# Mask rows of batch 1 from one pair's rows, and another order of work behind the opening

## The chip, the cores and the metric

The kernel runs on one core of a Trainium2 chip. The core has a matmul engine (PE, whose weight loads the profile lists apart as PEld), VectorE (DVE), ScalarE (ACT), GpSimd (POOL) and SyncE (SP), which issues the DMA transfers. Each engine works through its own queue in order and waits on semaphores for the others. PE writes its results to PSUM; DVE and ACT read them from there, GpSimd works in SBUF only. The metric is the device time of one execution in microseconds (us), the median of several runs.

## The reference

The computation is a block-sparse attention followed by a feed-forward layer. There are 4 batches, 8 heads, 768 positions and 64 columns per head, in 24 blocks of 32 positions:

```python
scores = scale * np.matmul(q, k.transpose(0, 1, 3, 2))
mask = np.abs(blk_i - blk_j) <= window            # window = 1
mask = mask | (blk_i == 0) | (blk_j == 0) | (blk_i == n_blocks - 1) | (blk_j == n_blocks - 1)
for qb in range(n_blocks):
    for kb in sampled_blocks[qb]:
        mask[qb*block:(qb+1)*block, kb*block:(kb+1)*block] = True
attn = softmax(np.where(mask, scores, -1e9))
x = (attn @ v)                                    # as 3072 rows of 512
h = x @ w_in                                      # 1024 columns
solu = h * softmax(h)
ln = (solu - mean) / sqrt(var + 1e-6) * g_ln
out = ln @ w_out                                  # 3072 x 512
```

The mask is the same for all batches and heads.

## The kernel before

**Tiling.** The heads are taken in four pairs. For each batch `b`, three query tiles `t` of 256 rows and each pair, `attend` makes three scores (each of four matmuls with 256 columns, called parts below), three exponentials on ACT of 128x1024 (L557), and one `pv` of 24 matmuls into an accumulator bank of PSUM (`mbank`, two banks); DVE takes reciprocals (L581) and writes the normalised rows (`norm`, L584). When four pairs of a tile are there, the rows are turned (`turn_x`, by a transposing DMA, `cross_x`, or on PE) and two row tiles of 128 go through `feed`: eight matmuls with `w_in` (L631), an exponential with its sum (L651), the product `us` (L654), statistics on DVE (L661, L664), a turn by DMA (`cross_u`, L738), eight matmuls with `w_out` (L748) and a scale (L758) that empties the accumulator bank into `ots`, which is stored. Row tiles are numbered through, from 0 to 23.

**The mask** is part of the matmul. kT and qT, the turned k and q, have 64 rows of data and 24 more rows (`MC`): for k, which block a column belongs to; for q, a negative number for each block that its row must not see. There are two kT and two qT, for even and odd batches. Batch 0's mask rows come with its turns on PE, pair by pair. Batch 1's were copied from batch 0's by two DMAs of SBUF to SBUF (`m1dma`, L800 for k and L801 for q), 24 partitions of 12,288 bytes each, when all four pairs' turns of batch 0 are copied out of PSUM. Batches 2 and 3 write only the data rows, so the mask rows stay.

**k, q and v.** In batch 0 k and q are cast to bf16, turned on PE and copied out by DVE or ACT (the opening). In later batches (`crossed`) a pair's k or q is loaded in float32, cast to bf16 (`cast6`, L270), turned by a DMA (`cross_kq`, L523) and put into kT or qT by two copies on DVE (`split`, L270). v is loaded and cast (`cast6`, L270).

**The weights.** w_in is loaded in four quarters (two for each half of its columns) and cast in eight pieces (`wcast`). w_out is loaded in two halves; `wg` (L425) multiplies its rows by the gain vector, which PE has turned (L407) and one copy has put into `g_sb`; PE sums those (L434), and eight folds `wo` (L439) write the final w_out.

**The order.** No loop sets the order of the work. The program first collects 1149 steps, each with its engine, what it depends on and which buffers it takes and frees; then the list `ORDER` puts all of them in one row, and `ENGINES` moves some steps to another engine than the default. Each engine issues its own steps in that order, and waits where its operands or its buffer are not there. Buffers (`take`) are given out in that order too, so a step that comes earlier can take another buffer. 26 `spare` matmuls on constants fill PE in the opening.

Of the kernel before, what the change touches and what calls it, by code (L numbers as in the profile page):

```python
# [11 lines left out]
ACT = mybir.ActivationFunctionType  # L12
# [7 lines left out]
    "ACT": [9, 24, 127, 291, 543, 1070, 1072, 1114, 1118, 1121],  # L20
    "DVE": [89, 92, 93, 95, 96, 126, 134, 135, 143, 161, 162, 165, 389, 393, 412, 420, 622, 626, 630, 639, 653,
        863, 868, 885, 886, 1116],
# [114 lines left out]
def kernel(  # L137
# [11 lines left out]
    nc = tc.nc  # L149
# [3 lines left out]
    NB = S // BLK  # L153
    NR = sampled_blocks.shape[1]
    P = 128
    NCH = S // P
# [696 lines left out]
```

## Time and profile before

| | |
|---|---|
| Median of 3 runs | 207.79 us (207.52 to 208.26) |
| Profiled execution | 206.38 us, with a span of 204.4 us from its first to its last instruction |
| PE busy | 198.4 us (97%) |
| ACT busy | 174.0 us (85%) |
| DVE busy | 149.9 us (73%) |
| GpSimd busy | 58.0 us (28%) |
| Granted PE clock | 1.00 |
| DMA | 43.17 MB, mean 211 GB/s |

A busy engine in this table is one with an instruction in it; matmuls are pipelined, so a busy PE is not PE at its peak. In rows of the profile, "out<-in" are names of buffers, "x24" is a count, and the brackets at the end of a row give the idle time before it and what ended it. A row of SP is the issue of a transfer, not the transfer. Times in rows count from the start of the span.

### The profile page before, as it was taken

To read this page: it belongs to the slowest core of one execution; us is meant where nothing else is said; L and a number is where in the kernel's file an instruction comes from. 1 tells how busy PE (TensorE), PEld (TensorE's weight loads), DVE (VectorE), ACT (ScalarE), POOL (GpSimd) and SP (SyncE) were. 2 spreads that over 40 slices of the span, in tenths; PEclk is the share of its full clock that TensorE was granted. 3 is DMA by queue.
4 is the path that set the end of the run, shared out by engine and by line. 5 is a ranking of instruction groups with operands and counts; after the bars stand their busy time and mean duration, and the time that the engine had idled before them with its cause. 6 is when DMAs were issued, how large, how long until landed. Compare 5 with 4: busy or idle time off the path is not lost.

```text
span 204.4 us, 5699 instructions
## 1 busy us (share of the span) xinstructions
PE 198.4 (97%) x2269; PEld 141.3 (69%) x2298; DVE 149.9 (73%) x341; ACT 174.0 (85%) x219; POOL 58.0 (28%) x132
## 2 busy tenths in 40 slices
PE   8999999999999999999999999999999999999993
PEld 4689886777657768667767777667677686675452
DVE  3488697999979648959776776599849736686771
ACT  4699999988998999999899899979998997775751
POOL 5705403430133024222303415025040110032160
PEclk9999999999999999999999999999999999999999
DMA  5999999989999999889999989999970921327524
GB/s 141 327 373 362 386 380 265 145 137 246 197 215 322 265 247 228 170 192 256 224 274 228 289 203 275 154 232 228 235 211 5 211 45 32 74 103 157 154 81 180
DMA packets 72214, 43.17 MB, mean 211 GB/s; under 512 B 53316, under 2 KB 67148, under 8 KB 72140
## 3 DMA queue, kind: packets, MB, share of 16 engines
q1 hardware_dynamic: 72152, 42.81, 86.8%
q8 instruction: 18, 0.29, 0.6%
q14 instruction: 8, 0.07, 0.1%
q10 hardware_dynamic: 36, 0.00, 0.0%
HBM read 23.07 MB, written 6.29 MB: 144 GB/s over the span
## 4 chain that ended last, share of the span: by engine, by line
PE 82%; DVE 9%; DMA 4%; issue 1%; POOL 1%; ACT 0%; POOLq 0%; SPq 0%; DVEq 0%
PE s L551 26%; PE mbank L748 17%; PE h L631 15%; PE mbank L572 15%; PE h L464 3%; DMA qx<-qb 2%; DVE us L654 2%; PE h L812 2%; DMA vst<-in_v_dram 2%; DVE w_out_sb L439 1%; PE mbank L812 1%; DVE ots L758 1%; DVE ex L425 1%; PE mbank L771 1%; DVE qT L270 1%
## 5 line engine op out<-in xcount | busy, mean ns | idle before, releaser
L557 ACT ACTIVATE ex<-s 128x1024 bf16<-128x1024 f32 x144 | 141.0, 1025 | 16.1 <-PE s L551 13.8
L551 PE MATMUL s<-qT,kT 88*128 88x256 bf16 x576 | 82.8, 272 | 0.2
L551 PEld LDWEIGHTS <-kT 88*128 88x128 bf16 x576 | 52.8, 97 | 20.9 <-issue 0.5
L748 PE MATMUL mbank<-w_out_sb,uTs 128*128 128x512 bf16 x171 | 45.4, 379 | 0.6
L631 PE MATMUL h<-w_in_sb,xT 128*128 128x512 bf16 x170 | 45.2, 378 | 0.7
L572 PEld LDWEIGHTS <-ex 128*128 128x128 bf16 x1152 | 40.9, 97 | 4.1 <-DVE ots L758 0.5
L572 PE MATMUL mbank<-va,ex 128*128 128x65 bf16 x1152 | 42.3, 193 | 0.3 <-DVE ots L758 0.2
L654 DVE TENSOR_TENSOR us<-h,e 128x1024 bf16<-128x1024 f32 x22 | 26.9, 1221 | 4.5 <-ACT e L651 4.3
L661 DVE BATCH_NORM_STATS2 bs<-us 128x6 f32<-128x512 bf16 x44 | 28.9, 682 | 0.2
L631 PEld LDWEIGHTS <-xT 128*128 128x128 bf16 x192 | 18.5, 97 | 13.9
L748 PEld LDWEIGHTS <-uTs 128*128 128x128 bf16 x184 | 17.3, 97 | 13.1
L758 DVE TENSOR_SCALAR ots<-mbank,rs 128x512 f32<-128x512 f32 x22 | 16.4, 746 | 11.1 <-POOL rs L703 4.5
L651 ACT ACTIVATE e<-h 128x1024 bf16<-128x1024 f32 x22 | 22.6, 1029 | 1.3 <-POOL vr L670 1.3
L581 DVE RECIPROCAL r<-mbank 128x4 f32<-128x4 f32 x48 | 8.1, 172 | 21.1 <-PE mbank L572 20.9
L670 POOL TENSOR_SCALAR vr<-z,mv 128x1 f32<-128x1 f32 x22 | 6.4, 293 | 58.2 <-DVE mv L664 50.5
L584 DVE TENSOR_TENSOR x<-mbank,r 128x256 bf16<-128x256 f32 x48 | 20.1, 421 | 1.2
L703 POOL TENSOR_TENSOR rs<-vr,neg_half 128x1 f32<-128x1 f32 x24 | 13.9, 579 | 1.5
L270 POOL CAST kb<-kst 128x768 bf16<-128x768 f32 x8 | 6.8, 854 | 21.4 <-DMA kst<-in_k_dram 19.8
L270 POOL CAST qb<-qst 128x768 bf16<-128x768 f32 x8 | 6.9, 858 | 11.9 <-DMA qst<-in_q_dram 10.4
L270 POOL CAST va<-vst 128x768 bf16<-128x768 f32 x8 | 6.8, 850 | 11.8 <-DMA vst<-in_v_dram 9.8
L667 POOL TENSOR_TENSOR z<-z 128x1 f32<-128x1 f32 x22 | 4.3, 197 | 19.0 <-ACT e L651 19.0
L270 DVE COPY kT<-kc 64x768 bf16<-64x768 bf16 x24 | 8.3, 348 | 0.6 <-DMA kc<-kb 0.3
(109 smaller groups left out, 133.8 us busy)
## 6 DMA issues: line engine op xcount, KB each, us to landing
vst<-in_v_dram SPq DMA_DIRECT2D x16, 384.0 KB, 4.9
out_dram<-ots SPq DMA_DIRECT2D x23, 256.0 KB, 2.3
kst<-in_k_dram SPq DMA_DIRECT2D x15, 384.0 KB, 5.7
qst<-in_q_dram SPq DMA_DIRECT2D x12, 384.0 KB, 5.6
w_out_f<-in_moe_w_out_dram SPq DMA_DIRECT2D x2, 1024.0 KB, 11.2
qst<-in_q_dram SPq DMA_DIRECT2D x4, 256.0 KB, 7.3
uTs<-in_moe_w_in_dram SPq DMA_DIRECT2D x2, 512.0 KB
ots<-in_moe_w_in_dram SPq DMA_DIRECT2D x2, 512.0 KB, 7.2
```

The source lines that it names most:

```text
L270: (nc.vector if o.eng == "DVE" else nc.gpsimd).tensor_copy(out=dst, in_=src)
L551: nc.tensor.matmul(s[:, m, :], kT[i][0:KR, pr, jc, hh, :], qT[i][0:KR, pr, 2 * t : 2 * t + 2, hh, :], start=(m % 2 == 0), stop=(m % 2 == 1))
L557: exs.append(op("exp", "ACT", lambda o, so=so: nc.scalar.activation(out=exb[o.slot], in_=lay["s"][so.slot], func=ACT.Exp, scale=scale), [s ...
L572: nc.tensor.matmul(acc(o)[:, qt, hh, :], exb[exs[n].slot][:, m, qt * P : (qt + 1) * P], va[i][:, 2 * pr + hh, jc, :], start=first, stop=(n ...
L584: nrm = op("norm", "DVE", lambda o: nc.vector.tensor_tensor(out=xb[x_of[b, t].slot][:, :, 2 * pr * D : (2 * pr + 2) * D].rearrange("p a (h ...
L631: nc.tensor.matmul(hx(n), xTb[xt[0].slot][:, qt, c, :], w_in_sb[n][:, c, :], start=(c == 0), stop=(c == KD - 1))
L651: zs = op("silu_e", "ACT", lambda o: nc.scalar.activation(out=eb[o.slots["e"]], in_=lay["h"][0].rearrange("p a f -> p (a f)"), func=ACT.Ex ...
L654: us = op("mult", "DVE", lambda o: nc.vector.tensor_mul(out=ub[o.slot], in0=lay["h"][0].rearrange("p a f -> p (a f)"), in1=eb[zs.slots["e" ...
L661: bs.append(op("stats", "DVE", lambda o, n=n: nc.vector.bn_stats(out=bsb[(bs[0] if bs else o).slot][:, n, :], in_=ub[us.slot][:, w(o, n)]) ...
L703: rs = op("rs", "POOL", lambda o: nc.gpsimd.tensor_tensor(out=rsb[o.slot], in0=vrb[vr.slot], in1=neg_half, op=ALU.pow), [vr, c2], take="rs ...
L748: nc.tensor.matmul(mbank[m0.slot], uTb[ut[0].slot][:, KF // 2 * n + f, :], w_out_sb[n][:, f, :], start=(n == 0 and f == 0), stop=(n == 1 a ...
L758: nc.vector.tensor_scalar(out=otb[o.slot], in0=mbank[os_[0].slot], scalar1=rsb[rs.slot], scalar2=None, op0=ALU.mult)
```

## The change

It has three parts.

1. **The mask copies.** Both still have 288 KB to write. The source is now only the first pair's rows, read four times (a broadcast over the pairs), so each copy has 96 runs of 3,072 bytes instead of 24 of 12,288. The k copy waits for the two copies out of PSUM of the first pair's k, the q copy for the first pair's two and for the mask step, not for all pairs'.
2. **Engines.** 18 steps go from DVE to GpSimd: four of the w_in casts, two casts of batch 0's q, three v casts of batch 0, and nine casts of later batches (among them batch 1's first q and its v of pairs 0 and 3). Ten go from GpSimd to DVE: three w_in casts, two casts of batch 0's q, and five of later batches (among them batch 1's first k and its v of pair 2). The copy of the gain vector and the scales of row tiles 14, 15 and 19 go from DVE to ACT, the last scale from ACT to DVE.
3. **The order** from the 81st of 1149 steps to the 624th. Behind that it is the same. The number of steps and of PE instructions does not change.

SP's queue shows most of the new order. From the load of batch 0's last q on it was: w_in quarter (second half), w_in quarter (first), v of pair 3, w_in quarter (first), w_in quarter (second), both w_out halves, then batch 1: q0, k0, k1, k2, q1, **mask q**, q2, turns of k0 and q0, turn of x tile 1, turn of q1, **mask k**, turn of k1, turn of us 1, loads k3, q3, turns of q2, k2, turn of us 2, **load v0**, turn of x tile 2, turn of k3, turn of q3, loads v1, v2, v3. It is now: w_in quarter (first), v of pair 3, w_out half (chunks 4 to 7), w_in quarters (first, second, second), other w_out half, then batch 1: k0, k1, q0, q1, k2, turn of k0, load q2, turns of q0 and of x tile 1, **mask k, mask q**, turn of q1, load k3, turn of k1, load q3, turn of us 1, turns of q2, k2, turn of us 2, turn of k3, turn of x tile 2, **load v0**, turn of q3, loads v1 and v2, and, behind a k load of batch 2 and the turn of us 3, v3.

On DVE, the w_out folds stand behind the reciprocal and norm of the first batch's pv (tile 1, pair 2) instead of around them; the statistics' closing steps come later. On PE the gain vector's turn comes ahead of the score of pair 2 and some scores change places; the kinds and numbers of matmuls are the same.

```diff
 ENGINES = {
     "POOL": [7],
-    "ACT": [9, 24, 127, 291, 543, 1070, 1072, 1114, 1118, 1121],
-    "DVE": [89, 92, 93, 95, 96, 126, 134, 135, 143, 161, 162, 165, 389, 393, 412, 420, 622, 626, 630, 639, 653,
-        863, 868, 885, 886, 1116],
+    "ACT": [9, 24, 100, 127, 291, 543, 811, 826, 1032, 1070, 1072, 1114, 1118],
+    "DVE": [86, 87, 89, 90, 126, 135, 153, 168, 385, 411, 412, 626, 657, 867, 876, 885, 886, 1116],
 }
 ORDER = [
...
-    1134, 97, 178, 135, 137, 138, 1141, 139, 140, 144, 26, 181, 42, 189, 1133, 179, 30, 29, 146, 145, 187, 148,
-    190, 188, 153, 185, 147, 1125, 36, 162, 186, 150, 149, 194, 151, 38, 143, 43, 44, 163, 196, 195, 191, 39,
+    1134, 97, 178, 135, 137, 138, 1141, 139, 140, 144, 26, 29, 145, 98, 181, 42, 30, 153, 189, 179, 146, 1125,
+    190, 187, 147, 148, 185, 36, 38, 1133, 188, 43, 44, 99, 149, 150, 162, 186, 194, 163, 39, 164, 195, 151, 143,
...
-            mask1["k"] = op("m1dma", "SP", lambda o: nc.sync.dma_start(out=kT[1][MC], in_=kT[0][MC]), kdone)
-            mask1["q"] = op("m1dma", "SP", lambda o: nc.sync.dma_start(out=qT[1][MC], in_=qT[0][MC]), qdone + [mq0])
+            for nm, t, done in (("k", kT, kdone[:2]), ("q", qT, [qdone[0], qdone[NPR], mq0])):
+                mask1[nm] = op("m1dma", "SP", lambda o, t=t: nc.sync.dma_start(
+                    out=t[1][MC].rearrange("r a c h p -> r a (c h p)"),
+                    in_=t[0][MC, 0:1].rearrange("r a c h p -> r a (c h p)").broadcast_to([NB, NPR, NCH * 2 * P])), done)
```

98 rows, old and new, of the table ORDER are left out of this document.

## The prediction

> **What bounds the kernel now.** I read the page first, then the engines by stage, then what PE waits for. The page:
>
> ```profile
> span 204.4 us, 5699 instructions
> PE 198.4 (97%) x2269; PEld 141.3 (69%) x2298; DVE 149.9 (73%) x341; ACT 174.0 (85%) x219; POOL 58.0 (28%) x132
> ```
>
> The busy time by stages (columns: stretch, length, then each engine's busy time):
>
> ```profile
> 7.00:30.00 23.00, 22.91 (x348) 20.36 (x351) 18.48 (x50) 21.25 (x23) 8.70 (x14) 1.00 1.05 369
> 30.00:62.00 32.00, 31.58 (x339) 21.84 (x344) 29.04 (x60) 29.63 (x37) 8.72 (x16) 1.00 1.05 208
> 62.00:96.00 34.00, 33.52 (x399) 24.00 (x401) 25.61 (x58) 31.58 (x39) 10.13 (x21) 1.00 1.06 235
> 96.00:180.00 84.00, 83.25 (x981) 59.64 (x993) 59.70 (x133) 74.96 (x89) 19.72 (x44) 1.00 0.82 182
> ```
>
> PE never rests for long, at a granted clock of 1.00. From 30 to 62 us DVE and ACT are at 29 of 32 as well; behind that DVE falls to 60 of 84. The PE instructions are the same before and after, so the change can win only what PE waits behind the opening, and lose whatever new waits it makes. Those waits (what PE's weight loads wait for, total, times, longest):
>
> ```profile
> PEld L572 <- DVE ots L758: 0.5, 1, 0.5
> PEld L551 <- DVE kT L270: 0.3, 1, 0.3
> PEld L572 <- issue: 0.3, 1, 0.3
> PEld mbank L407 <- issue: 0.2, 1, 0.2
> ```
>
> They sum to 1.3 us: hardly more can be won.
>
> **The change, part by part.**
>
> *DVE from 34 to 57 us.* Two of the waits are for DVE, so its queue is the term. Two weight folds (L439) stretched under GpSimd casts, and two casts that leave DVE:
>
> ```profile
> 36.11 0.55 DVE L270 CAST qb<-qst 128x768 bf16<-128x768 f32 x1
> 37.23 1.31 DVE L439 SCALAR_TENSOR_TENSOR w_out_sb<-w_out_f,g_sb,wbar 128x512 bf16<-128x512 f32 x1
> 36.90 1.10 POOL L270 CAST qb<-qst 128x768 bf16<-128x768 f32 x1 [0.97 <-DMA qst<-in_q_dram]
> 39.61 1.16 DVE L439 SCALAR_TENSOR_TENSOR w_out_sb<-w_out_f,g_sb,wbar 128x512 bf16<-128x512 f32 x1
> 39.40 0.83 POOL L270 CAST kb<-kst 128x768 bf16<-128x768 f32 x1 [1.41 <-DMA kc<-kb]
> 43.72 0.72 DVE L439 SCALAR_TENSOR_TENSOR w_out_sb<-w_out_f,g_sb,wbar 128x512 bf16<-128x512 f32 x1
> 57.21 0.56 DVE L270 CAST va<-vst 128x768 bf16<-128x768 f32 x1 [0.32 <-DMA vst<-in_v_dram]
> ```
>
> A fold takes 0.72 alone, 1.31 and 1.16 under a cast: 0.59 + 0.44 = 1.03 lost. Both ended 0.54 behind the cast's end (38.54 against 38.00, 40.77 against 40.23): the cast made them wait. Batch 1's first q cast (0.55) goes to GpSimd, its first k cast comes to DVE earlier, in this hole:
>
> ```profile
> 31.68 0.18 DVE L581 RECIPROCAL r<-mbank 128x4 f32<-128x4 f32 x1 [1.28 <-PE mbank L572]
> 35.50 0.69 DVE L661 BATCH_NORM_STATS2 bs<-us 128x6 f32<-128x512 bf16 x1
> 35.88 0.88 PEld L572 LDWEIGHTS <-ex 128*128 128x128 bf16 x24
> ```
>
> The hole of 1.28 covers it (0.55); without the hole it would cost 0.55. In the new order DVE takes a reciprocal right behind these statistics, which end at 36.19; it needs the pv whose weight loads end at 36.76 and whose result comes a little later, with the folds queued behind. That is 0.7 of new idle time. Sum: -0.55 - 1.03 + 0.7 = -0.9 if no fold meets a cast. Two k/q casts of batch 1 (pairs 2) now fall on GpSimd near 40 us, by the landing of their transposes; each that meets a fold costs 0.44 to 0.59. I take one, the middle of none and two: DVE is 0.4 earlier, with ends 0.9 earlier and 0.1 later (a third collision counts another 0.5).
>
> *The wait at 56.94.* The last splits of pair 2, and what PE does:
>
> ```profile
> 56.17 0.72 DVE L270 COPY kT<-kc 64x768 bf16<-64x768 bf16 x2
> 55.97 0.64 PEld L748 LDWEIGHTS <-uTs 128*128 128x128 bf16 x4
> 56.94 0.33 PEld L551 LDWEIGHTS <-kT 88*128 88x128 bf16 x4 [0.33 <-DVE kT L270]
> 59.03 0.64 PEld L631 LDWEIGHTS <-xT 128*128 128x128 bf16 x4
> 59.78 0.53 PEld L551 LDWEIGHTS <-kT 88*128 88x128 bf16 x4
> ```
>
> The splits end at 56.89, 0.4 earlier would be 56.5. PE needs about 0.11 to turn from a 512-column group to a score (59.67 to 59.78), so of 0.33 some 0.2 can go: **-0.2** (ends -0.2 and +0.1).
>
> *The wait at 62.84.* A pv waits for an accumulator bank that DVE empties late (scale of row tile 1):
>
> ```profile
> 61.09 0.99 PEld L572 LDWEIGHTS <-ex 128*128 128x128 bf16 x24
> 62.03 0.75 DVE L758 TENSOR_SCALAR ots<-mbank,rs 128x512 f32<-128x512 f32 x1
> 62.84 0.78 PEld L572 LDWEIGHTS <-ex 128*128 128x128 bf16 x24 [0.48 <-DVE ots L758]
> ```
>
> Ahead of that scale the v cast of 57.21 (0.56) leaves DVE, and DVE starts 0.4 earlier: it ends near 61.8 instead of 62.78, while PE, 0.2 ahead and with one more score (about 0.35) in front of that pv, arrives near 62.5. **-0.47** (ends -0.47 and 0). What is late next is v itself, the first rival below.
>
> *The other two waits.* The gain vector's turn (L407) moves ahead into the opening, where PE waits anyway for DVE and ACT: 0, ends -0.2 and 0. The 0.3 at L572 near 42 us: DVE and ACT meet there in both orders: 0, ends -0.3 and +0.3.
>
> *Gain vector's copy on ACT.* 0.17 on DVE:
>
> ```profile
> 22.05 0.17 DVE L270 COPY g_sb<-mbank 128x8 f32<-128x8 f32 x1 [1.07 <-PE mbank L407]
> 44.38 2.85 ACT L557 ACTIVATE ex<-s 128x1024 bf16<-128x1024 f32 x3 [0.85 <-PE s L551]
> ```
>
> ACT is at 21.25 of 23 up to 30 us, so some 0.2 may show there, but at 44.38 ACT has 0.85 to spare: 0, ends 0 and +0.2 without that cover.
>
> *w_in and w_out loads and casts.* One w_out half now loads ahead of three w_in quarters, four w_in casts go from DVE to GpSimd and three come back. The bytes in front of batch 1's loads are the same. GpSimd's price:
>
> ```profile
> L270 POOL CAST w_in_sb<-ots 128x512 bf16<-128x512 f32 x3 | 1.8, 614 | 3.0 <-PE h L464 2.3 <-DMA ots<-in_moe_w_in_dram 0.7
> ```
>
> Four such casts now run beside DVE's casts for the first feed and may hold one of them for most of 0.61; the hole of 1.28 comes only behind that feed. 0, since DVE has the three casts in front of its last w_out products, ends 0 and +0.4.
>
> *Mask copies.* Two transfers:
>
> ```profile
> 26.55 0.87 SPq L801 DMA_DIRECT2D qT<-qT  x1
> 42.17 0.78 SPq L800 DMA_DIRECT2D kT<-kT  x1
> 47.48 1.04 PE L551 MATMUL s<-qT,kT 88*128 88x256 bf16 x8
> vst<-in_v_dram SPq DMA_DIRECT2D x16, 384.0 KB, 4.9
> ```
>
> Both now issue behind the transpose of x tile 1, near 38 to 41 us; a 384 KB load lands in 4.9, so these 288 KB are there by 46, ahead of the first score of batch 1 (47.48). The bytes stay; fewer sources to wait for changes nothing, because the q copy, waiting for all pairs, was already issued at 26.55. SP still pays two issues (0.87 and 0.78). 0, ends -0.1 and +0.3; past 47.5 each us of delay would be a us of PE.
>
> *Late parts.* Three scales (0.75 each on DVE) go to ACT late in the run, where ACT has time to spare (74.96 of 84): 0, end +0.3. The last scale goes from ACT to DVE:
>
> ```profile
> 199.27 0.75 DVE L758 TENSOR_SCALAR ots<-mbank,rs 128x512 f32<-128x512 f32 x1 [0.50 <-PE mbank L748]
> 201.15 0.47 ACT L779 ACTIVATE ots<-mbank,rs 128x256 f32<-128x256 f32 x1 [0.54 <-PE mbank L771]
> ```
>
> Half of DVE's columns take about 0.42 (estimate from 0.75 for 512 and a fixed part): **-0.05**, ends -0.1 and 0. Behind 62 us six casts leave DVE and four come; DVE has 8 us to spare in 34 there, so 0.
>
> *Sum.* -0.2 - 0.47 - 0.05 = -0.7. The profiled execution took 206.38 (2.0 around its span of 204.4), 1.4 below the median of the three runs, 207.79; it becomes 205.7, and the median 207.1.
>
> One rule speaks against the change. The Trainium skill (SBUF — State Buffer, Who interferes with whom) says that VectorE and GpSimd share a port pair under an exclusive lock, and that whoever starts first holds it for the whole instruction while the other blocks. The two folds that ended 0.54 behind their casts agree with it. By it, every cast moved to GpSimd can hold DVE for its whole 0.83 instead of the 0.5 I count, and with two such on the folds the sum would be near 0 instead of -0.7.
>
> **The rivals.**
>
> *Slower: v of batch 1 comes late.* SP's queue here:
>
> ```profile
> 53.26 0.57 SPq L353 DMA_DIRECT2D vst<-in_v_dram  x1
> 54.01 1.24 SPq L614 DMA_TRANSPOSE xT<-x  x1
> 55.35 1.26 SPq L523 DMA_TRANSPOSE kc<-kb  x1
> ```
>
> The first v load of batch 1 moves behind these two transposes, which wait for DVE's casts, splits and norms. Its cast now sits on GpSimd, in order, and others wait behind it. With everything else in place it issues at 53.26 + 2.5 = 55.8, lands 4.9 later at 60.7, and is cast (0.83) at 61.5; PE wants it at 60.9. I count on the transposes' issuing about 1 us earlier, because DVE is earlier: issue 54.6, cast by 60.4. It costs from an issue at 55.2 on (60.9 - 0.83 - 4.9), eats the whole gain of 0.7 at 55.9, and is worth +0.6 at 56.5: 208.4. For it: DMA is full here (1.05 of its engines). Against: before, that v was cast at 57.77, 3.3 us ahead of PE.
>
> *No change: the collisions eat DVE's lead.* Two or three folds and products meet casts, DVE is 0.2 to 0.7 late at the splits, and the wait at 56.94 grows by as much as the one at 62.84 loses; or feed 0 is 0.4 late. 0 to -0.2: 207.7. For it: DVE at 29.04 of 32. Against: fewer casts on DVE.
>
> *The mask copies matter by themselves.* If the 26.55 copy held up the loads and transposes of batch 1, up to 1 us of DVE's start would come forward; but PE could win only the waits above, 1.3 in all: 206.5. It is the low end.
>
> **How the numbers follow.** Forecast (both DVE waits shortened) 0.44, with the mask case in it; no change 0.22; slower 0.34, by late v mostly, since PE, ACT, DVE and SP are all nearly full from 30 to 62 us and any of them being late costs. About 0.3%, 0.6 us, is what a measurement of this kernel can tell from no change; 207.1 lies just past it, so faster 0.44, same 0.22, slower 0.34. The range goes from 206.4 (all 1.3 won and 0.1 of the end) to 208.7 (late v); the likeliest case alone is 206.5 to 207.5.
>
> **What would show it.** Right: no wait of PE for L758 near 62 us, the splits of pair 2 done by 56.7, folds at 0.7 each, the last pv groups of stage 62 about 0.7 earlier, and the rest shifted by the same. Wrong: weight loads of pv waiting for GpSimd's va or for DMA of vst near 61 us; folds at 1.1 and more; a feed waiting for w_in_sb near 29 us; a score waiting for the mask copies near 47 us.

## The result, and the profile after

The change made the kernel 0.8% slower: 208.99 us in the median of 11 runs (208.10 to 210.19) against 207.52 of the kernel before (206.99 to 208.26), a ratio of 1.0078, 95% interval 1.0058 to 1.0098. The forecast was 207.1; the rival "v of batch 1 comes late" stood at 208.4. In one experiment below ("v first") five of six runs had a granted clock of 0.989 to 0.991, where all other runs had 0.996 to 1.000, so only its profiled execution is read.

The page of the changed kernel (its profiled execution took 209.43):

```profile
span 207.1 us, 5698 instructions
PE 197.7 (95%) x2269; PEld 140.6 (68%) x2298; DVE 145.2 (70%) x330; ACT 175.1 (85%) x222; POOL 64.0 (31%) x140
```

GpSimd took over 6.0 us of work and DVE lost 4.7, as the change says. PE has the same matmuls in a span that is 2.7 us longer. By stages (stretch, length, then each engine's busy time):

```profile
30.00:62.00 32.00, 31.15 (x317) 21.07 (x321) 28.38 (x59) 29.01 (x36) 9.01 (x16) 1.00 1.01 188
62.00:96.00 34.00, 32.35 (x388) 23.33 (x390) 22.16 (x47) 30.39 (x38) 12.71 (x25) 1.00 1.10 247
96.00:180.00 84.00, 82.82 (x976) 59.07 (x989) 58.68 (x132) 76.58 (x93) 18.78 (x42) 1.00 0.84 183
```

PE was busy for less time in each of these stages (31.58, 33.52 and 83.25 before), so it waited more. What PE's weight loads wait for:

```profile
PEld L571 <- issue: 1.9, 2, 1.4
PEld L550 <- DVE kT L269: 0.7, 1, 0.7
PEld L630 <- issue: 0.5, 1, 0.5
PEld L747 <- DMA uTs<-us: 0.4, 1, 0.4
PEld L571 <- DVE ots L757: 0.2, 1, 0.2
```

Most line numbers are one lower than before. The wait for the scale (L757) fell from 0.48 to 0.2, much as forecast; the others stand at other places than before, or are new. "Issue" at L571 is PE waiting in a pv; PE's matmul row and GpSimd's rows give the reason:

```profile
65.27 1.62 PE L571 MATMUL mbank<-va,ex 128*128 128x65 bf16 x48 [1.44 <-POOL va L269]
```

```profile
38.40 1.00 POOL L269 CAST qb<-qst 128x768 bf16<-128x768 f32 x1 [2.61 <-DMA qx<-qb]
39.35 1.28 POOL L269 CAST kb<-kst 128x768 bf16<-128x768 f32 x1
...
60.91 0.82 POOL L269 CAST va<-vst 128x768 bf16<-128x768 f32 x1 [4.56 <-DMA vst<-in_v_dram]
...
64.39 0.82 POOL L269 CAST va<-vst 128x768 bf16<-128x768 f32 x1 [1.50 <-DMA vst<-in_v_dram]
```

The pv of pair 1 waited for the cast of its v, and the cast for its load. This v had little to spare before the change: GpSimd's cast ended at 62.72, and PE started that pv at 62.84.

```profile
61.90 0.82 POOL L270 CAST va<-vst 128x768 bf16<-128x768 f32 x1 [0.59 <-DMA vst<-in_v_dram]
```

SP's queue in the changed kernel, which issues that load:

```profile
37.42 1.24 SPq L613 DMA_TRANSPOSE xT<-x  x1
38.76 1.28 SPq L800 DMA_DIRECT2D kT<-kT  x1
40.15 0.78 SPq L800 DMA_DIRECT2D qT<-qT  x1
41.02 4.13 SPq L522 DMA_TRANSPOSE kc<-qb  x1
...
47.83 1.96 SPq L737 DMA_TRANSPOSE uTs<-us  x1
...
57.04 0.57 SPq L352 DMA_DIRECT2D vst<-in_v_dram  x1
57.71 1.21 SPq L522 DMA_TRANSPOSE kc<-qb  x1
58.98 1.10 SPq L352 DMA_DIRECT2D vst<-in_v_dram  x2
```

The transpose behind the two mask copies held SP for 4.13 us. It did not wait for its data: GpSimd had cast its q by 35.8. The same transpose before (the one at 40.88, ahead of the k copy):

```profile
40.88 1.24 SPq L523 DMA_TRANSPOSE kc<-qb  x1
42.17 0.78 SPq L800 DMA_DIRECT2D kT<-kT  x1
43.05 2.07 SPq L523 DMA_TRANSPOSE kc<-kb  x1
45.22 1.46 SPq L738 DMA_TRANSPOSE uTs<-us  x1
```

And the first VectorE product that PE waits for, before the change:

```profile
49.59 1.23 DVE L654 TENSOR_TENSOR us<-h,e 128x1024 bf16<-128x1024 f32 x1
```

From 41.02 to 61 us SP of the changed kernel issues without a pause, and the kernel before had none over 0.24 us there either. So part of the 2.9 us is handed on: the turn of product 1 issues 2.6 later than before, the load of v of pair 1 1.0 later. This load lands at 64.34, before the change at 61.85. Of these 2.5 us only 1.0 is the later issue; the other 1.5 it spent on the way (5.36 from issue to landing, before 3.86). In the trace the copies' 192 packets of 3,072 bytes, 0.26 us each in the median, start from 40.92 to 45.62; if all 16 DMA engines share them evenly, which the trace does not tell, that is 192 x 0.26 / 16 = 3.1 us of each.

The third place is in batch 2 (VectorE, GpSimd, PE's weight loads):

```profile
107.23 0.75 DVE L757 TENSOR_SCALAR ots<-mbank,rs 128x512 f32<-128x512 f32 x1 [0.27 <-POOL rs L702]
107.90 1.24 DVE L269 COPY kT<-kc 64x768 bf16<-64x768 bf16 x2
```

```profile
107.15 1.78 POOL L269 CAST va<-vst 128x768 bf16<-128x768 f32 x2
```

```profile
109.19 0.22 PEld L550 LDWEIGHTS <-kT 88*128 88x128 bf16 x3 [0.71 <-DVE kT L269]
```

Two splits took 1.24 beside the second of two v casts (108.07 to 108.93). Before the change they took 0.73, from 105.37 on; GpSimd did one of these casts behind them, at 107.05, and DVE the other, at 108.14.

To see where the time goes I take the lag: how much later a step of PE starts than the same step in the trace of the kernel before (the first weight load of each). It is one execution each, so a column is read downwards. The columns, experiments all but the first: the old form of the copies; the copies ahead of the first k transpose of batch 1; that with one v cast of batch 2 on DVE; that with the v casts of batch 1 as before; all mended; mended with one feed set back; two v casts of batch 2 on DVE alone; and their exchange alone.

| PE's step, its time before | changed | old form | copies first | + one cast | + v casts | mended | feed back | two casts | swap |
|---|---|---|---|---|---|---|---|---|---|
| score, batch 1, 49.93 | 0.05 | -0.12 | -0.16 | -0.16 | -0.53 | -0.16 | -0.22 | -0.11 | -0.77 |
| w_out group of row tile 1, 54.67 | 0.77 | 0.43 | 0.31 | -0.12 | -0.06 | 0.31 | -0.22 | 0.44 | -0.44 |
| pv of pair 0, 61.09 | 0.76 | 0.74 | 0.54 | 0.11 | 0.16 | 0.53 | 0.47 | 0.53 | 0.17 |
| pv of pair 2, 63.98 | 1.99 | 1.33 | 0.18 | -0.26 | -0.21 | 0.16 | 0.10 | 0.72 | 0.55 |
| score, batch 2, 105.87 | 1.97 | 1.31 | 0.16 | -0.28 | -0.23 | 0.14 | 0.34 | 0.72 | 0.54 |
| feed of row tile 10, 106.85 | 2.58 | 1.93 | 0.78 | 0.07 | 0.35 | 0.24 | 0.44 | 0.82 | 0.63 |
| w_out group of row tile 9, 111.44 | 2.58 | 1.93 | 0.78 | 0.07 | 0.34 | 0.72 | 0.92 | 1.30 | 0.63 |
| last group, 198.80 | 2.57 | 1.92 | 0.77 | 0.05 | 0.32 | 0.72 | 0.93 | 1.31 | 0.63 |
| end of the span | 2.76 | 2.12 | 0.96 | 0.25 | 0.51 | 0.72 | 0.92 | 1.50 | 0.82 |

This execution of the changed kernel loses 0.72 at 50 to 55 us, 1.23 at the pv near 64, 0.61 at 107 and 0.19 at the end: 2.75 of the span's 2.76. The other columns are the experiments below. This execution is 0.4 above the changed kernel's median and the one before 1.1 below its own; the medians differ by 1.5.

How much of a loss is chance can be read from four executions of what is one program up to the casts at 105 us: "changed", "two casts", "swap", and the experiment with one cast moved, which has no column. They are 1.1 us apart in the first row already, and from the pv of pair 0 to that of pair 2 their lag grows by 1.23, 0.19, 0.38 and 1.40. The load of v of pair 1 was on its way for 5.4, 4.4, 4.4 and 5.6 us in them. With the copies ahead of the first k transpose the lag falls there instead, by 0.36 or 0.37 in each of six traces, though that load was on its way for 3.8 to 5.5. So the sign of this loss is sure, and 1.23 is near its upper end; what sets a load's time on the way stays open. The loss at 107 us hardly varies: 0.61 or 0.62 in the five traces without an edit there.

### The profile page after: what moved, and what is told of

The parts are those of the page before. It is cut to its first block, busy times and chain, and to the rows that moved or that the text cites. A ratio compares the mean times of both kernels' runs of the same rounds, so it can differ in the third digit from the quotient of the medians.

```text
span 207.1 us, 5698 instructions
## 1 busy us (share of the span) xinstructions
PE 197.7 (95%) x2269; PEld 140.6 (68%) x2298; DVE 145.2 (70%) x330; ACT 175.1 (85%) x222; POOL 64.0 (31%) x140
## 4 chain that ended last, share of the span: by engine, by line
PE 78%; DVE 8%; DMA 5%; SPq 2%; issue 2%; ACT 2%; POOL 1%; DVEq 0%; POOLq 0%; ACTq 0%
PE s L550 25%; PE h L630 16%; PE mbank L571 15%; PE mbank L747 15%; DVE w_out_sb L438 3%; DMA vst<-in_v_dram 3%; DMA kst<-in_k_dram 2%; PE h L463 2%; ACT ex L556 1%; DVE us L653 1%; SPq L352 1%; PE mbank L770 1%; DVE bs L660 1%; DVE kT L269 1%; PE s L630 1%
## 5 line engine op out<-in xcount | busy, mean ns | idle before, releaser
L747 PE MATMUL mbank<-w_out_sb,uTs 128*128 128x512 bf16 x173 | 45.6, 379 | 0.7
L571 PEld LDWEIGHTS <-ex 128*128 128x128 bf16 x1152 | 40.9, 97 | 5.1 <-issue 1.9
L571 PE MATMUL mbank<-va,ex 128*128 128x65 bf16 x1152 | 42.2, 194 | 1.6 <-POOL va L269 1.4
L757 DVE TENSOR_SCALAR ots<-mbank,rs 128x512 f32<-128x512 f32 x19 | 14.1, 744 | 7.2 <-issue 4.3
L269 POOL CAST qb<-qst 128x768 bf16<-128x768 f32 x11 | 9.2, 840 | 13.8 <-DMA qst<-in_q_dram 7.5
L269 POOL CAST va<-vst 128x768 bf16<-128x768 f32 x11 | 9.1, 831 | 13.0 <-DMA vst<-in_v_dram 12.9
L269 DVE COPY kT<-kc 64x768 bf16<-64x768 bf16 x24 | 9.6, 400 | 0.4
L269 POOL CAST kb<-kst 128x768 bf16<-128x768 f32 x9 | 7.9, 875 | 4.9 <-DMA kst<-in_k_dram 4.8
```

The costliest lines, as they stand in the source:

```text
L269: (nc.vector if o.eng == "DVE" else nc.gpsimd).tensor_copy(out=dst, in_=src)
L571: nc.tensor.matmul(acc(o)[:, qt, hh, :], exb[exs[n].slot][:, m, qt * P : (qt + 1) * P], va[i][:, 2 * pr + hh, jc, :], start=first, stop=(n ...
L747: nc.tensor.matmul(mbank[m0.slot], uTb[ut[0].slot][:, KF // 2 * n + f, :], w_out_sb[n][:, f, :], start=(n == 0 and f == 0), stop=(n == 1 a ...
L757: nc.vector.tensor_scalar(out=otb[o.slot], in0=mbank[os_[0].slot], scalar1=rsb[rs.slot], scalar2=None, op0=ALU.mult)
```

## The experiments

Theory: the two mask copies put together in front of the transposes of pair 1 hold SP's queue, and the losses up to 64 us follow from it; GpSimd's casts beside DVE's splits cost the 0.6. Rivals: the copies' new form; the engines of the v casts; DVE's or PE's new order. All ratios are to the kernel before, on the chip of the run.

**The form of the copies.** The changed kernel with the old copies, and the kernel before with the new ones (the diff of the change's last part, backwards in the one and alone in the other).

> The changed kernel with the old mask copies (24 runs of 12 KB each, from all pairs), at their new places behind the transpose of x tile 1 and with the new order and engines. Chain theory (two copies together are what holds the queue, in whatever form): the transpose behind them still takes 3 to 5 us to issue and the time is 208.5 to 209.5. Rival (the 96 runs hold the queue): the transpose issues in 1.2 to 2.1 and the time falls to 207.0 to 208.

> The kernel before with only the mask copies changed (96 runs of 3 KB each from pair 0's rows, waiting for pair 0 alone), at their old places on SP and with the old order and engines. Chain theory: the form costs little where the copies stand apart (26.55 and 42.17): 207.3 to 207.9, ratio within 0.3% of 1. Rival (the form itself, four times the descriptors, is what holds the queue): the transpose behind the copy at 42.17 takes 3 us and more to issue instead of 2.07, and the time is 208.2 to 209. Second rival (the form is what helps, as the short runs spread over all DMA engines): the transposes behind issue in 1.24 and the time is 206.5 to 207.

Old form in the changed kernel: ratio 1.0102 (1.0076 to 1.0128), and the transpose behind the copies still takes 3.82 (4.13). New form alone: 1.0000 (0.9981 to 1.0018). So the form does nothing to the time that shows. 48 packets of 12,288 bytes take 1.0 us each in the median, 48 x 1.0 / 16 = 3.0 us of each engine on the same assumption, as much as the 192 short ones.

**The place of the copies.** First both ahead of the load of q of pair 2, which in the new order stands behind the first k transpose of batch 1, then both ahead of that transpose:

```diff
+for _i, _j in ((174, 53), (175, 53)): ORDER.remove(_i); ORDER.insert(ORDER.index(_j), _i)
```

> The changed kernel with both mask copies moved back on SP's queue only, to just behind the k load of pair 2 of batch 1, where SP was idle from 26.3 to 32.5 us. Chain theory: in the changed kernel the transpose behind the two copies took 4.13 us to issue (41.02 to 45.15) where such a transpose takes 1.24, and all that follows on SP is late by that. Without the copies in front of it it takes 1.2 to 1.7, the first v load of batch 1 issues at 54.2 to 55.2 instead of 57.04, and PE's wait for va at 63.7 (1.8 us) is at most 0.5: 206.9 to 207.9, against 208.99 of the changed kernel. Rival (the engines of the casts, not SP, make it slow): the transpose issues faster but the v loads still wait for DVE's work in front of them, 208.5 to 209.2. Second rival (DMA is full at 26 us): the copies hold back the loads and transposes of batch 1 by up to 2 us, 208.5 or more, with the first splits of batch 1 later.

```diff
+for _i, _j in ((174, 386), (175, 386)): ORDER.remove(_i); ORDER.insert(ORDER.index(_j), _i)
```

> The changed kernel with both mask copies moved ahead of the first k transpose of batch 1 on SP (not behind it, as in the earlier trial), where SP idled from 26.3 to 32.5 us; nothing else moves. The copies' 3.1 us of all DMA engines then fall behind the loads, at 32 to 36 us, and not in front of the transposes of pair 1. Queue theory: the transpose of q pair 1 issues by 41 in 1.2 to 1.7, the turn of product 1 issues at 45 to 46 instead of 47.83, the first v load by 55.5, and the losses of 0.77 at 50 to 55 us and of 1.2 at 63.7 shrink to at most 0.3 and 0.3; the 0.6 of batch 2 stays. About 207.2 on the chip of the first trials (before 206.66 there), ratio to before 1.000 to 1.005. Rival (DMA is the bound here and the copies cost the same 3 us in front of whatever stands behind them): the first k and q transposes of batch 1 land at 39 to 41 instead of 36 to 38, SP is as late at 48 us as in the changed kernel, ratio 1.006 to 1.010.

The first gave 1.0059 (1.0037 to 1.0081): the copies issued at 34.4, not at 26 as I had written, and now the two transposes behind them took 3.02 and 2.60 to issue; the first v load stayed at 57.06. I had expected 0.5 us of wait at most and a v load at 54.2 to 55.2, so this missed; but it shows that the delay sits on whatever transposes stand behind the copies. The second gave 1.0051 (1.0032 to 1.0070), just past the upper end of what the queue theory allowed. Its SP queue:

```profile
34.83 2.96 SPq L522 DMA_TRANSPOSE qx<-qb  x1
37.89 1.79 SPq L613 DMA_TRANSPOSE xT<-x  x1
39.77 1.99 SPq L522 DMA_TRANSPOSE kc<-qb  x1
...
44.37 1.27 SPq L737 DMA_TRANSPOSE uTs<-us  x1
...
55.05 0.57 SPq L352 DMA_DIRECT2D vst<-in_v_dram  x1
```

The turn of product 1 issues 3.5 earlier than in the changed kernel, the v load 2.0, and in the table ("copies first") the loss at the pv near 64 is gone: the lag even falls from 0.54 to 0.18. The 3 us are still paid, by the first transposes (k's lands at 39.24, in the changed kernel at 35.95, before the change at 39.26), but SP has pauses behind them, at 45.6 and at 49.3, and the delay ends there. By the ratios a third of the loss goes (1.0051 for 1.0078, on different chips), by the lags from the first row on 1.6 of 2.7 us. One part of the theory failed: up to the pv of pair 0 the lag grows by 0.70, as in the changed kernel (0.71). That loss does not come from the copies.

**v first.** The changed kernel with two v loads ahead of the k transpose of pair 3:

```diff
+for _i, _j in ((48, 413), (51, 413)): ORDER.remove(_i); ORDER.insert(ORDER.index(_j), _i)
```

> The changed kernel with the first two v loads of batch 1 put ahead of the k transpose of pair 3 (issued 54.40) on SP; nothing else moves. Chain theory: they issue near 54.4 and 55.0 instead of 57.04 and 58.98, land near 59 and 60, GpSimd casts them by 61 and the wait of pv of pair 1 at 63.7 (1.8 us) is gone; the 0.77 that was lost at 50 to 55 us and the 0.6 of batch 2 stay: 207.4 to 208.2. Rival (the transposes of pair 3 that now come 1.2 later are as urgent): the splits of pair 3 wait, the score of pair 3 at 62.8 is late by 0.5 to 1.2, and the time stays at 208.5 to 209.2.

The ratio is 1.0192 (1.0131 to 1.0252), and the profiled execution, the only one that is read here, took 208.78. The v casts end at 57.95 and 60.05 and the pv waits no more, as the chain theory said. But DVE, and PE behind it:

```profile
59.01 0.36 DVE L269 COPY kT<-kc 64x768 bf16<-64x768 bf16 x1 [1.87 <-DMA kc<-kb]
59.40 1.23 DVE L653 TENSOR_TENSOR us<-h,e 128x1024 bf16<-128x1024 f32 x1
```

```profile
60.67 1.02 PE L630 MATMUL h<-w_in_sb,xT 128*128 128x512 bf16 x4 [1.49 <-DVE us L653]
```

DVE waited 1.87 for the transpose now behind the loads, the product queued behind that split was late, and a feed waited 1.49 for it. The rival was right in kind: SP's queue has no pause there, and what goes ahead is paid by what falls back.

**One cast of batch 2.** The changed kernel with v of pair 1 of batch 2 on DVE; then that together with the copies ahead of the first transpose; then also the v casts of batch 1 as before.

```diff
+for _i, _e in ((639, "DVE"),): [_k.remove(_i) for _k in ENGINES.values() if _i in _k]; ENGINES[_e].append(_i)
```

> The changed kernel with one cast, v of pair 1 of batch 2, back on DVE as before; order and all else as changed. In the changed kernel two v casts ran on GpSimd one after the other at 107.15 to 108.93, the split beside the second took 0.87 instead of 0.35, and PE lost 0.6 at 108.4. Collision theory: the split takes 0.35, PE waits at most 0.1 there, and 0.6 of the 2.57 us goes: ratio to before 0.003 lower than the changed kernel's, about 1.005 to 1.007. Rival (the split was late for another reason, its DVE queue): PE still waits 0.5 or more there, and the ratio stays at 1.0078 to 1.010.

> The two edits above together: copies ahead of the first k transpose of batch 1, and v of pair 1 of batch 2 on DVE. If the three losses are separate, they add: all of the 2.57 us but 0.3 to 0.6 goes, ratio to before 0.997 to 1.003. If one loss hides another (a PE that comes earlier waits for the next late piece), the sum falls short by half and the ratio is 1.003 to 1.006.

> The kernel with both edits and besides the v casts of pairs 0, 2 and 3 of batch 1 on the engines of before (DVE, GpSimd, DVE). Theory that GpSimd's cast of v is part of the late chain: PE's wait for va at 63.7 goes, ratio 0.2 to 0.4% below that of the kernel with both edits. Rival (the v load's landing is what is late, whichever engine casts it): DVE, which works in order, now waits itself for the landing near 59 us, the product of feed 3 or a scale behind it is late, and the ratio is the same or 0.2 to 0.6% above.

Alone: 1.0095 (1.0063 to 1.0126), no gain, where 1.005 to 1.007 was expected. The other v cast, that of pair 2, still ran beside the split, later by its load, and the two splits took 1.24 again. With the copies: 1.0029 (1.0006 to 1.0052); with the v casts too 1.0006 (0.9989 to 1.0024). So with the copies out of the way and these four casts set back, the changed kernel is level with the one before, as far as the medians tell. The step from 1.0029 to 1.0006 lies within the intervals, and the lag at 63.98 is the same in both (-0.26 and -0.21): that GpSimd's cast of v costs by itself is not shown, and the late landing is enough to explain the wait.

**The collision by itself.** Both v casts on DVE; then the two casts with places and engines exchanged, so that GpSimd's ends before the splits start.

```diff
+for _i, _e in ((639, "DVE"), (648, "DVE")): [_k.remove(_i) for _k in ENGINES.values() if _i in _k]; ENGINES[_e].append(_i)
```

> The changed kernel with v of pairs 1 and 2 of batch 2 on DVE and nothing else. With one of them moved back, the other one still ran on GpSimd beside the split at 108.4. Collision theory: now the two splits take 0.7 in place of 1.24, PE's lag does not grow from 1.97 to 2.58 at that place, the ratio is 0.003 below the changed kernel's (1.005 to 1.007). Rival (the split is late for another reason): the lag still grows by 0.6 there and the ratio is 1.0078 to 1.010.

```diff
+for _i, _j in ((648, 639),): ORDER.remove(_i); ORDER.insert(ORDER.index(_j), _i)
+for _i, _e in ((648, "DVE"),): [_k.remove(_i) for _k in ENGINES.values() if _i in _k]; ENGINES[_e].append(_i)
```

> The changed kernel with this swap of the two v casts of batch 2 alone. Collision theory: PE's lag stays at its value of 105 us (1.97 in the changed kernel's profile) to the end, the ratio is 0.003 below the changed kernel's 1.0078 to 1.010, that is 1.005 to 1.007. Rival: another wait of 0.4 or more in its place and the ratio of the changed kernel.

Both on DVE: 1.0093 (1.0069 to 1.0117). The splits took 0.73 together and the lag grew by 0.10 at 107, not by 0.61, so the collision was its cause, though the ratio missed the expected 1.005 to 1.007: 0.48 came back at the next pv:

```profile
106.65 0.73 DVE L269 COPY kT<-kc 64x768 bf16<-64x768 bf16 x2
...
111.44 0.55 DVE L269 CAST va<-vst 128x768 bf16<-128x768 f32 x1
```

```profile
PE mbank L571 <- DVE va L269: 0.3, 1, 0.3
```

Exchanged: 1.0055 (1.0034 to 1.0077), and nothing comes back (the table's last column). GpSimd, VectorE and PE's weight loads:

```profile
105.72 0.82 POOL L269 CAST va<-vst 128x768 bf16<-128x768 f32 x1
```

```profile
106.46 0.73 DVE L269 COPY kT<-kc 64x768 bf16<-64x768 bf16 x2
```

```profile
107.25 0.22 PEld L550 LDWEIGHTS <-kT 88*128 88x128 bf16 x3 [0.20 <-DVE kT L269]
```

GpSimd's cast ends at 106.54, as the splits start. In the traces the collision is a cost of its own of 0.5 us, and it is a matter of a microsecond of timing. The ratio fell as expected, but its interval still overlaps with that of the changed kernel.

**All mended, and PE's order.** The copies ahead of the first transpose, the v casts of batch 1 as before, both v casts of batch 2 on DVE, the last half scale on ScalarE; then the same with the first matmuls of feed 3 behind the next score; then the mended kernel with the two v casts of batch 2 exchanged, as above, and not both on DVE.

```diff
+for _i, _j in ((174, 386), (175, 386), (340, 461)): ORDER.remove(_i); ORDER.insert(ORDER.index(_j), _i)
+for _i, _e in ((639, "DVE"), (648, "DVE"), (393, "DVE"), (411, "POOL"), (420, "DVE"), (1121, "ACT")): [_k.remove(_i) for _k in ENGINES.values() if _i in _k]; ENGINES[_e].append(_i)
```

> The changed kernel with the copies ahead of the first k transpose of batch 1, the v casts of pairs 0, 2 and 3 of batch 1 on the engines of before, v of pairs 1 and 2 of batch 2 both on DVE, and the last half scale on ScalarE as before. Against the trial with both edits and the v casts (ratio 1.0006, span 0.5 above before's): the split near 106 us takes 0.35 instead of 0.87 as no GpSimd cast runs beside it, which gives back 0.57; the last scale starts 0.04 behind its matmul instead of 0.21, which gives back 0.17. Collision theory: span 0.2 to 0.3 below before's, ratio 0.996 to 0.999. Rival (two casts of 0.55 on DVE at 108 to 110 delay the reciprocal and the product behind them): PE waits as much for them, ratio 1.000 to 1.003.

> The mended kernel with one step of PE's order set back: the first matmuls of feed 3 behind the next score (as before the change), not ahead of it. In all kernels with the new order PE waits there for the product of feed 2, which VectorE ends at the same time as before (50.8), and loses 0.4 to 0.65 at 50 to 51 us. Theory that this order is what lost there: that loss is gone, and 0.3 to 0.6 of it stays to the end: ratio 0.993 to 0.997. Rival (the next waits, for the turn of product 1 and for the splits at 56.9, take what is gained, as VectorE sets the pace): ratio as in the mended kernel within 0.001.

> As the mended kernel (copies ahead of the first k transpose, v casts of batch 1 and the last half scale as before), but of the two v casts of batch 2 that of pair 1 is on GpSimd, where it ends before the splits start, and that of pair 2 on DVE at the place of the other, ahead of its pv. Collision theory: splits 0.35 each, no wait of pv for the cast, PE's lag does not grow between 105 and 114 us: 0.5 to 0.6 less than the mended kernel's (ratio 1.0018), so 0.998 to 1.000. Rival (the place is full, whichever piece is moved): another wait of 0.4 or more at 106 to 114 us, ratio 1.001 to 1.003.

The diff is that of the second; the first lacks the pair (340, 461), the third has (648, 639) for it and no 639 on DVE. Mended: 1.0018 (0.9998 to 1.0037), where 0.996 to 0.999 was expected; with the feed set back 1.0021 (1.0000 to 1.0041); with the exchange 1.0016 (0.9994 to 1.0037). None beats the kernel before. For the exchange 0.998 to 1.000 was expected: in its trace the lag indeed grows by 0.09 only from 105.87 to the last group (mended: 0.58), but the medians do not show these 0.5 us. With the feed set back the loss of 0.47 at 50 to 55 us is gone ("feed back": -0.22 and -0.22), and comes back two steps later:

```profile
57.15 0.11 PEld L550 LDWEIGHTS <-kT 88*128 88x128 bf16 x2 [0.76 <-DVE qT L269]
```

The rival was right, as far as this one step goes: VectorE sets the pace there, and the order of PE only chooses where PE waits for it. What would take this loss away was not found.

**The k copy early in the kernel before**, with the new form of both copies, next to the q copy at 26.55, which the shorter list of sources allows; and **the last half scale on DVE** in the kernel before:

```diff
+for _i, _j in ((174, 53),): ORDER.remove(_i); ORDER.insert(ORDER.index(_j), _i)
```

> The kernel before with the new form of the mask copies, and the k copy moved on SP from 42.17 to directly behind the q copy at 26.55, which the shorter list of sources allows; order and engines else as before. Queue theory: the copies' 3.1 us of DMA, 1.5 of them at 43 to 45 us in front of the k transpose of pair 1, go to 34 to 37 us; that transpose issues in 1.2 instead of 2.07 and the turn of product 1 behind it up to 0.9 earlier. PE waits at 56.94 and 62.84 for DVE, not for SP, so at most 0.2 to 0.5 of it shows: ratio 0.997 to 1.000. Rival (the first k transpose then lands later than 39.3 and its splits, 44.4 to 46.9 on DVE, are late): ratio 1.002 to 1.006.

```diff
+for _i, _e in ((1121, "DVE"),): [_k.remove(_i) for _k in ENGINES.values() if _i in _k]; ENGINES[_e].append(_i)
```

> The kernel before with the last half scale on DVE instead of ScalarE. By the forecast's term the end comes 0.05 earlier; by the trace of the changed kernel (it started 0.21 behind the modelled end of the matmul on DVE, 0.04 on ScalarE, and took 0.49 against 0.47) 0.17 later. Either is too little for the ratio, which is 0.999 to 1.002; the profile shows the start and the duration.

The k copy early: 0.9992 (0.9974 to 1.0011), no difference that shows. The last scale: 0.9995 (0.9972 to 1.0018), and in the profile

```profile
200.86 0.48 DVE L781 TENSOR_SCALAR ots<-mbank,rs 128x256 f32<-128x256 f32 x1 [1.18 <-PE mbank L771]
```

0.48 and not the 0.42 of the estimate. In this trace the last group of PE is 0.35 earlier than before and the end 0.27: the move costs 0.08. In the changed kernel it cost 0.19; with the scale on ScalarE (mended) the lag does not grow there at all.

## Why the prediction was wrong

The forecast added three gains to a row of zeros. Of the gains only the one at 62.84 came, and in part. Of what stood at zero, or was not costed at all, three things were losses: the mask copies, PE's new places at 50 us, and the casts behind 62 us.

- *Mask copies, "0, ends -0.1 and +0.3".* This is the step that failed first. I asked only when the copies land: by 46, ahead of the score at 47.48. The last of their packets ended at 45.95, and no score waited. What I left out is what stands behind them: a transpose whose issue then took 4.13 instead of 1.24, on a queue without a pause for 20 us. I had counted their issues (0.87 and 0.78) alone. With v behind them PE's lag grew by 0.19 to 1.40 up to the pv of pair 2; with the copies ahead of the first k transpose it fell by 0.36. The row that could have told it was in the trace of before: the k transpose behind the one copy took 2.07.
- *"Issue 54.6" of the v load.* It issued at 57.04, past the 55.2 from which it was to cost. I took the transposes in front of it as 1 us earlier, because DVE would be; they were later, because SP was. The rival had the place, the mechanism and the sign; it priced issue at 56.5 at +0.6; in the trace that issued at 57.04 the pv lost 1.23, part of it by chance of the load's time on the way. Its pair was not the one that waited: v of pair 0 was ready at 61.73, and PE, itself 0.76 late, came for it at 61.85. The forecast's "3.3 us ahead of PE" was the slack of pair 0; that of pair 1, two issues further on, was 0.12.
- *DVE 0.4 earlier.* It was not. Two GpSimd casts at 38.40 to 40.63 met the folds, four of which took 3.86; with the copies first, where no cast met them, they took 2.73:

```profile
37.31 3.86 DVE L438 SCALAR_TENSOR_TENSOR w_out_sb<-w_out_f,g_sb,wbar 128x512 bf16<-128x512 f32 x4
...
49.61 1.22 DVE L653 TENSOR_TENSOR us<-h,e 128x1024 bf16<-128x1024 f32 x1
```

  The product of row tile 2 starts at 49.61, before the change at 49.59. Two collisions and not one, the bad end of my range, and with them the lead is zero. Each cost 0.56, as I had counted for one. The Trainium skill (SBUF — State Buffer, Who interferes with whom) has the later of the two wait for the other's whole instruction; the trace agrees in kind, as both folds ended 0.54 behind their casts, but the price was not the 0.83 that I took from it.
- *The wait at 62.84, -0.47.* Right in kind: it fell to 0.18. The pv then stood at v for 1.45; without that the lag at the pv of pair 2 would be 0.54, 0.2 less than at that of pair 0, and with the copies first 0.36 to 0.37 were won there. All of 0.47 was not to be had, with the cast of this v ending 0.12 ahead of PE before the change.
- *The wait at 56.94, -0.2.* It went, but not because DVE was early (the splits ended at 57.72, not 56.5): PE came later, having waited at 50 us for the product and at 54.2 for the turn of product 1. The new places of feed 3 and of scores, which I mentioned as "some scores change places" and did not cost, made 0.72 of new waits. With SP on time they are 0.47 there, but 0.7 again at the pv of pair 0, and the feed set back only moves them.
- *"DVE has 8 us to spare in 34 there, so 0"* for the casts behind 62 us. Spare time over a stage says nothing about which pieces meet: one split met a cast and PE lost 0.6 at 107 us.
- *Last scale, -0.05.* +0.08 to +0.19 in single traces. Small, and of the other sign; the ratio shows nothing of it.
- *Right:* the form of the copies, the gain vector's turn and copy, the weights' loads and casts. No feed waited for w_in near 29 us, and the lag at the end of the opening (28.3 us) is 0.07.

Not settled: how the copies hold the issue of a transpose. That the transpose's issue ended at 45.15, when the copies' last packets were starting (45.62), was seen; whether it waits for room in a queue or for something else, no run here tells.

## What to carry to other kernels

A transfer has two prices: when it lands, and how long it keeps what is behind it on its queue. Where a DMA-issuing queue has no pause, the second is handed on to loads far behind: of 2.9 us here, 2.6 reached the next turn and 1.0 a load 18 us later, which had next to nothing to spare. So the slack to look up is that of every load on the queue, not of the first. And an order that keeps the pieces of two engines apart by timing alone is undone by a shift of one microsecond: an average of spare time doesn't cover a collision.

## What the runs showed of the hardware

- Two copies within SBUF that write 288 KB each, on 24 partitions, have as much packet time in 48 packets of 12,288 bytes (1.0 us each in the median) as in 192 of 3,072 (0.26). The transposing DMA directly behind the two took 3.78 to 4.13 us to issue, instead of 1.24, in the six kernels with the copies at the new place; with the copies ahead of the first k transpose the delay fell on three transposes from 34 us on (2.96, 1.79 and 1.99 in one kernel, 4.62, 1.76 and 1.97 in another).
- A split of 64x768 bf16 takes 0.35, and 0.87 beside a GpSimd cast that started before it; the scale of 107.23, which reads PSUM, took its usual 0.75 beside the same casts. The Trainium skill (SBUF — State Buffer, Who interferes with whom) has it so: a VectorE copy in a mode that takes two SBUF ports and a GpSimd instruction shut each other out for the whole instruction, while an instruction with at most one SBUF input outside those modes does not contend. The trace agrees, though no row shows in which mode the split ran: it ended at 109.14, 0.21 behind the cast.
- A half scale of 128x256 out of PSUM takes 0.48 on VectorE and 0.47 on ScalarE, but VectorE's starts later behind the last matmul (its end is modelled): at 203.89 behind 203.68 in the changed kernel and at 200.86 behind 200.76 in the last experiment, where ScalarE's before the change starts at 201.15 behind 201.11. These are single traces.
